# Four gate and value blocks of the first unit summed up before its scaling is known, and weight pieces 2 and 3 decoded earlier

## The chip, the cores and the metric

The kernel runs on one core of a Trainium2 chip. The metric is the device time of one execution in microseconds (us). TensorE (PE in the profile) multiplies matrices, VectorE (DVE), ScalarE (ACT) and GpSimd (POOL) do elementwise work, and SyncE (SP) issues the DMAs. Each engine works through its own list of instructions in order and waits on the others by semaphores.

## The reference

Windowed attention over 8 batches x 8 heads x 576 positions x 64, then an MLP with a gate over the 4608 rows of the attention's output:

```python
scores = where(mask, scale * q @ k.T, -1e9)      # 32 keys back, or 32 keys back in steps of 4
x      = softmax(scores) @ v                     # laid out as 4608 x 512
rms    = sqrt(mean(x * x, -1) + 1e-6)
xn     = x / rms * rms_g
g      = xn @ w_gate                             # 512 x 1536
out    = (g * sigmoid(g) * (xn @ w_val)) @ w_out # 1536 x 512
```

The weights arrive as 64-bit numbers, so the kernel has to make 32-bit ones of them.

## The kernel before

**Units and steps.** The 4608 rows are worked off in 16 units of 288 (`u`), with the features across the partitions. A unit's attention has 14 blocks of scores, `(u, c, i)`: c is a pair of heads (0 to 3), i a block of queries. The MLP has 12 blocks of 128 features (`j`), each with three steps: `gate` (tile g), `val` (tile v) and `proj` (tiles acc0 to acc3). The program is a list of steps. The opening has 25 of them, n = 0 to 24, with the attention of unit 0 and the first scores of unit 1. Then follows the main loop, in which t counts steps within all units: t = 3j + part, and unit 0 begins with t = 2.

**The order of work.** It is written out by hand. `later(dt, rank, fn)` puts a function into the step dt further on; at the head of each step `flush` calls what was put there, sorted by rank, and the matmuls of the step follow. The order of the calls is the order on each engine: nothing is rearranged later, and an instruction that waits holds up everything behind it on its engine.

**Weight pieces.** Gate, value and output weights come as 36 blocks of 128 x 512; two make one piece m: m = 0 is g0 and v0, m = 1 is g1 and v1, m = 2 is o0 and g2, m = 3 is v2 and o1, m = 4 is g3 and v3. A piece is loaded (L152), then `rebase` scales its high words into a new tile f (on POOL, L164, for m < 3, on ACT, L166, from then on), and then DVE makes the bits right. For m < SIGNS these are three operations, `shift` (L172), `low` (L175) and `sign` (L179). From SIGNS on there are two, `rest` (L184) and `whole` (L188), and for them POOL first clears the high words but for their sign, in place (L169), after `rebase` has read them. STEPS gives how many of these DVE operations each opening step has, and REBASES the opening steps with a rebase; in unit 0's part of the main loop every step has one operation, but for t = PAUSE.

**Unit 0's scaling.** Of each row the root of the mean square is needed. ACT copies the attention's output into xraw_c (L426; DVE does it for two blocks of c = 3), squares it (L445), POOL multiplies xraw_c by rms_g (L447), and POOL or DVE adds up the squares (L451). PE then sums over partitions (rps, L551), DVE adds 1e-6 (L558), POOL takes the power (L559), DVE spreads it over a diagonal (rd, L583), PE broadcasts it (bps, L593), and DVE multiplies xraw into xn (L604) and copies the factor to `root` (L598). One block, j = 0, doesn't wait for that: `start` (steps in FIRST) sums its g and v over the unscaled xraw, and DVE applies the root to g before the tanh (L683) and to the product (L704). L684 is the tanh, L689 finishes the gate, L702 multiplies with v.

**PSUM.** g and v of block j lie in two banks that alternate: g of block j + 1 takes the bank of v of block j, and v of block j + 1 that of g. So a `gate` may begin only when DVE has read the last v but one, by L702. `busy` are matmuls without use (L765), which keep PE occupied in the opening.

Of the kernel before, what the change touches and what calls it, by code (L numbers as in the profile page):

```python
# [9 lines left out]
F32 = mybir.dt.float32  # L10
# [4 lines left out]
ALU = mybir.AluOpType  # L15
# [5 lines left out]
P = 128  # L21
U = S // 2
# [3 lines left out]
QB = 96  # L26
# [8 lines left out]


LAG, OUT, LATER = 4, 2, 1
STEPS = (0,) * 6 + (1, 0) * 2 + (1,) * 4 + (0,) * 9 + (2, 1)
REBASES = 5, 9, 21, 23
BUSY = 5, 2  # L40
SIGNS = 4
SPLITS = 5, 31, 35

PAUSE = 31

ORDER = [(0, 0, "q"), (0, 1, "q"), (0, 0, "v"), (0, 2, "q"), (0, 0, "w"), (0, 1, "v"), (0, 3, "qv"), (0, 2, "v"),
         (0, 0, "g"), (0, 0, "w"), (0, 0, "w"), (1, 0, "qv")]
SECOND = 14, 18, 22
ZEROS = 19, 23, 26
FIRST = {19: (("g", 0), ("g", 1)), 20: (("g", 2),), 22: (("g", 3), ("v", 0), ("v", 1)),  # L50
         23: (("v", 2), ("v", 3))}


SCORES = {1: (-3, -2, 0, 1, 3, 4, 6, 7, 9, 10, 12, 13, 15, 16),
# [20 lines left out]
def attn_moe(ctx: ExitStack, tc: tile.TileContext, qk_in, v_in, w_gate, w_val, w_out, rms_g, outT):  # L75
# [560 lines left out]
    def weight(kind, u, j):  # L636
        return wts[kind, j] if u else single(kind, j)

    def three(out, wt, cc, x, start, stop, late_lo=False):
        if not isinstance(x, tuple):  # L640
            PE.matmul(out, wt[:, cc, :], x, start=start, stop=stop)  # L641
            return
        (wh, wl), (xh, xl) = wt, x
        PE.matmul(out, wh[:, cc, :], xh, start=start, stop=False)  # L644
        rest = [(wh, xl), (wl, xh)]
        for k, (w, v) in enumerate(rest[::-1] if late_lo else rest):
            PE.matmul(out, w[:, cc, :], v, start=False, stop=stop and k == 1)  # L647

    first = {}

    def start(kind, c):

        if kind not in first:
            first[kind] = ps.tile([P, 512], F32, tag={"g": "acc1", "v": "acc3"}[kind], name=f"{kind}_0_0")
        three(first[kind][:, :U], weight(kind, 0, 0), c, xraw[0, c], c == 0, c == NC - 1)

    def bank(kind, j):
        return "gv"[(j + (kind == "v")) % 2]

    def group(kind, u, j):  # L660

        if u + j == 0:
            return first.pop(kind)
        out = ps.tile([P, 512], F32, tag=bank(kind, j), name=f"{kind}_{u}_{j}")
        for c in range(NC):
            three(out[:, :U], weight(kind, u, j), c, xs[u][c], c == 0, c == NC - 1)
        return out

    def gate(u, j):
        g_ps = group("g", u, j)
        if u == 0:
            used.append(("g", j))
        g = g_ps[:, :U]

        def tanh():
            nonlocal g
            t = (sb.tile([P, U], F32, tag="hhi", name=f"h_{j}", bufs=2) if u == 0 else
                 sb.tile([P, U], F32, tag="th", name=f"th_{u}_{j}", bufs=1))  # L680
            if u + j == 0:
                g = sb.tile([P, U], F32, tag="hhi", name="g_first", bufs=2)
                V.tensor_tensor(out=g, in0=g_ps[:, :U], in1=root[0], op=ALU.mult)  # L683
            A.activation(out=t, in_=g, func=AF.Tanh, scale=0.5)  # L684
            gv[u, j] = t

        def silu():
            t = gv[u, j]
            V.scalar_tensor_tensor(out=t, in0=t, scalar=1.0, in1=g, op0=ALU.add, op1=ALU.mult)  # L689

        later(1, 0 if u + j else 0.65, tanh)
        later(1, 0.8, silu)
        return g_ps[:, U:U + 2 * QB]

    def val(u, j):
        v_ps = group("v", u, j)
        if u == 0:
            used.append(("v", j))

        def prod():  # L700
            t = gv[u, j]
            V.tensor_tensor(out=t, in0=t, in1=v_ps[:, :U], op=ALU.mult)  # L702
            if u + j == 0:
                V.tensor_tensor(out=t, in0=t, in1=root[0], op=ALU.mult)  # L704

        def parts():
            t = gv.pop((u, j))
            if u == 0:
                hs[u, j] = t
                return  # L710
            hi = sb.tile([P, U], F32R, tag="hhi", name=f"hhi_{u}_{j}", bufs=2)
            lo = late[0].tile([P, U], F32R, tag="hlo", name=f"hlo_{u}_{j}", bufs=2)
            A.copy(out=hi, in_=t)  # L713
            (V if (u, j) == (NU - 1, NJ - 1) else G).tensor_tensor(out=lo, in0=t, in1=hi, op=ALU.subtract)  # L714
            hs[u, j] = (hi, lo)

        later(1 if u + j else 2, 0, prod)
        later(1 if u + j else 2, 0.5, parts)
        return v_ps[:, U:U + 2 * QB]
# [42 lines left out]
    def busy(n):  # L762

        for _ in range(n):
            PE.matmul(busy_ps, ones, ones[:, None, :].to_broadcast([P, 4, P]), start=True, stop=True)  # L765
# [31 lines left out]
    for n in range(ends):  # L797
        decode(STEPS[n])
        if n in REBASES:
            later(0, 8, ahead)  # L800
        flush()
        t_ps = None
        if "t" in events.get(n, {}):
            t_ps = ps.tile([P, 512], F32, tag="gv"[n % 2] if n < nb + LAG else "acc0", name=f"t_first_{n}")[:, :2 * QB]
        s_tags = ("s", "acc0", "acc1") if n < nb else ("s", "acc0") if n < nb + LAG + OUT else ("s", "acc2")
        attend(t_ps, s_tag=s_tags[n % len(s_tags)], o_tag=("o", "acc2")[n % 2])
        if n < nb + LAG + OUT:
            busy(0 if n < 2 else BUSY[1] if n < nb + LAG - 1 else 1)
        for kind, c in FIRST.get(n, ()):
            start(kind, c)  # L810
        if n == ends - 1:
            gate(0, 0)
            val(0, 0)
        now[0] += 1

    prev = None
    for u in range(NU):
        for j in range(NJ):
            for part in range(0 if u + j else 2, 3):
                t = 3 * (u * NJ + j) + part  # L820
                if used and (t >= SPLITS[2] or part == 2 and SPLITS[0] <= t < SPLITS[1]):
                    later(0, 6, lambda: split_weight(*used.pop(0), V if t < SPLITS[1] or t % 2 else G, t >= SPLITS[2]))
                if u == 0:
                    decode(t != PAUSE)
                    if t == PAUSE:
                        later(0, 8.9, ahead)
                opening = len(ops) <= 2
                flush()
                if opening and not late:
                    early.close()  # L830
                    late.append(ctx.enter_context(tc.tile_pool(name="late", bufs=2)))
                if part == 0:
                    free = gate(u, j)
                elif part == 1:
                    free = val(u, j)
                else:
                    if prev is not None:
                        proj(*prev)
                    prev = (u, j)
                    free = None  # L840
                    if "t" in events.get(now[0], {}):
                        free = ps.tile([P, 512], F32, tag=bank("g", j), name=f"t_{u}_{j}")[:, :2 * QB]
                attend(free, s_tag="acc2" if t < 4 else "s")
                now[0] += 1
    flush()
# [69 lines left out]
```

## Time and profile before

| | us |
|---|---|
| median of 3 runs | 1125.83 |
| the three runs | 1125.37, 1125.83, 1130.24 |
| the profiled execution | 1130.38 |
| its span, first to last instruction | 1128.6 |
| PE busy in it | 1115.5 (99%) |
| DVE, ACT, POOL busy | 781.5, 700.9, 602.3 |

In the profile, a row of the timeline is start, duration, engine, line, operation, output and input tiles, and in brackets how long the engine was idle before and what it had waited for. A matmul in 32-bit precision is two records. L numbers are lines of the kernel before; in the changed one all lines behind the table of constants stand one further down (two from the loop over the opening steps on).

### The profile page before, as it was taken

How to read it: one execution, taken by the hardware profiler on the slowest of the kernel's cores; microseconds unless marked ns; L12 is line 12 of the kernel's file. 1: busy time of each engine (PE TensorE's matmuls, PEld its weight loads, DVE VectorE, ACT ScalarE, POOL GpSimd, SP SyncE). 2: the span in 40 equal slices, each digit the busy share in tenths (PEclk: the TensorE clock that was granted, in tenths of full speed). 3: DMA queues.
4: the chain of work that ended last, by engine and by line, in shares of the span. 5: the costliest groups of instructions: out<-in, count | busy, mean ns of one | idle time of the engine just before them, and what ended most of it. 6: DMA issues, size and time to landing. Idle time of an engine off the chain costs nothing.

```text
span 1128.6 us, 25810 instructions
## 1 busy us (share of the span) xinstructions
PE 1115.5 (99%) x8362; PEld 1086.6 (96%) x8362; DVE 781.5 (69%) x2838; ACT 700.9 (62%) x2579; POOL 602.3 (53%) x1050
## 2 busy tenths in 40 slices
PE   8999999999999999999999999999999999999998
PEld 6787999999999999999999999999999999999998
DVE  7789768758687675867758587685867767586412
ACT  6696576757567575766757666575766757576311
POOL 7423576646566554655646556564655646475211
PEclk9899999999999999999999999999999999999999
DMA  9666212303122121311313122121312212120000
GB/s 246 165 226 228 71 43 61 96 27 98 42 76 67 31 82 40 93 52 41 93 30 91 39 74 62 36 85 39 96 42 60 82 34 80 42 80 15 6 17 21
DMA packets 61544, 82.19 MB, mean 73 GB/s; under 512 B 7298, under 2 KB 41090, under 8 KB 61410
## 3 DMA queue, kind: packets, MB, share of 16 engines
q1 hardware_dynamic: 61410, 80.54, 24.2%
q8 instruction: 67, 1.10, 0.4%
q14 instruction: 67, 0.55, 0.2%
HBM read 71.08 MB, written 9.44 MB: 71 GB/s over the span
## 4 chain that ended last, share of the span: by engine, by line
PE 93%; DVE 3%; DMA 2%; ACT 1%; issue 1%; POOL 0%; SPq 0%; POOLq 0%; DVEq 0%; ACTq 0%
PE acc L647 16%; PE g L647 16%; PE v L647 16%; PE acc L644 9%; PE v L644 9%; PE g L644 9%; PE s L506 3%; PE o L494 3%; PE acc L641 2%; PE v L641 2%; PE g L641 2%; PE o L495 1%; PE t L481 1%; PE o L490 1%; PE v L481 1%; PE g L481 1%
## 5 line engine op out<-in xcount | busy, mean ns | idle before, releaser
L714 POOL TENSOR_TENSOR hlo<-th,hhi 128x288 fp32r<-128x288 f32 x179 | 145.3, 812 | 198.2 <-ACT hhi L713 148.4
L647 PE MATMUL acc<-hhi,lo 128*128 128x288 f32 x720 | 212.4, 295 | 0.0
L409 POOL TENSOR_SCALAR t<-t,sum 72x72 f32<-72x72 f32 (+3 forms) x414 | 153.4, 382 | 75.6 <-DVE sum L403 62.9
L647 PE MATMUL g<-xhi,lo 128*128 128x288 f32 x612 | 180.3, 295 | 0.0
L647 PE MATMUL v<-xhi,lo 128*128 128x288 f32 x612 | 180.2, 294 | 0.0
L713 ACT CAST hhi<-th 128x288 fp32r<-128x288 f32 x180 | 78.1, 434 | 153.4 <-DVE th L702 150.4
L393 ACT ACTIVATE t<-t,sum 96x128 f32<-96x128 f32 (+3 forms) x448 | 166.1, 375 | 10.3 <-DVE sum L382 9.8
L684 ACT ACTIVATE th<-g 128x288 f32<-128x288 f32 x180 | 73.8, 410 | 107.4 <-PE g L647 89.3
L321 POOL TENSOR_TENSOR vlo<-vt,vhi 128x128 fp32r<-128x128 f32 x182 | 86.1, 473 | 101.3 <-ACT vhi L317 87.4
L647 PEld LDWEIGHTS acc<-hhi,lo 128*128 128x128 f32 x720 | 135.4, 188 | 0.0
L439 DVE TENSOR_TENSOR xraw<-o,xraw 64x72 f32<-64x72 f32 (+1 forms) x364 | 99.2, 273 | 50.4 <-ACT xraw L429 44.4
L689 DVE SCALAR_TENSOR_TENSOR th<-th,g 128x288 f32<-128x288 f32 x180 | 80.5, 447 | 71.4 <-ACT th L684 67.5
L647 PEld LDWEIGHTS g<-xhi,lo 128*128 128x128 f32 x612 | 115.1, 188 | 0.0
L647 PEld LDWEIGHTS v<-xhi,lo 128*128 128x128 f32 x612 | 115.1, 188 | 0.0
L644 PE MATMUL g<-xhi,hi_g 128*128 128x288 f32 x357 | 111.4, 312 | 0.8 <-DVE th L702 0.8
L644 PE MATMUL acc<-hhi,hi_o 128*128 128x288 f32 x360 | 110.7, 307 | 0.0
L702 DVE TENSOR_TENSOR th<-th,v 128x288 f32<-128x288 f32 x180 | 81.5, 453 | 38.0 <-PE v L647 30.0
L647 PE MATMUL acc<-hlo,hi_o 128*128 128x288 f32 x360 | 106.5, 296 | 0.0
L429 ACT COPY xraw<-o 64x72 f32<-64x72 f32 (+1 forms) x364 | 94.1, 258 | 11.7 <-PE o L495 9.6
L377 DVE TENSOR_TENSOR t<-s,mask 96x256 f32<-96x256 f32 (+3 forms) x182 | 66.8, 367 | 47.7 <-PE s L506 42.3
L351 POOL TENSOR_TENSOR ks<-qk,ks 128x288 fp32r<-128x288 f32 (+2 forms) x104 | 99.6, 973 | 0.0
L647 PE MATMUL g<-xlo,hi_g 128*128 128x288 f32 x322 | 94.9, 295 | 0.0
(192 smaller groups left out, 3565.5 us busy)
## 6 DMA issues: line engine op xcount, KB each, us to landing
qk<-in_qk_dram SPq DMA_DIRECT2D x60, 288.0 KB, 2.8
vt<-in_v_dram SPq DMA_DIRECT2D x196, 64.0 KB, 1.8
qk<-in_qk_dram SPq DMA_DIRECT2D x30, 352.0 KB, 3.1
out_dram<-ot SPq DMA_DIRECT2D x64, 144.0 KB, 1.9
qk<-in_qk_dram SPq DMA_DIRECT2D x30, 304.0 KB, 2.8
raw<-in_w_gate_dram SPq DMA_DIRECT2D x12, 512.0 KB, 6.1
raw<-in_w_val_dram SPq DMA_DIRECT2D x12, 512.0 KB, 5.2
raw<-in_w_out_dram SPq DMA_DIRECT2D x12, 512.0 KB, 4.2
```

The lines of the kernel that those rows point to most:

```text
L321: G.tensor_tensor(out=vl, in0=vs.pop(b), in1=vh, op=ALU.subtract)
L351: ek.tensor_tensor(out=ks[:, 1, :nkt], in0=kr, in1=ks[:, 0, :nkt], op=ALU.subtract)
L393: A.activation(out=t[:nq, a, :n], in_=t[:nq, a, :n], func=AF.Exp, scale=-1.0, bias=sm[:nq, a, 0:1], accum_out=sm[:nq, a, 1:2] if u or i % ...
L409: (V if u == 0 and (c, i) > (NC - 1, 0) else G).tensor_scalar(out=t[:nq, a, :n], in0=t[:nq, a, :n], scalar1=sm[:nq, a, 3:4], scalar2=1.0, ...
L429: A.copy(out=to[a * D:(a + 1) * D], in_=o[a * D:(a + 1) * D, (2 + a) * nq:(3 + a) * nq])
L439: V.tensor_tensor(out=to[rows], in0=o[rows, a * nq:(a + 1) * nq], in1=to[rows], op=ALU.add)
L644: PE.matmul(out, wh[:, cc, :], xh, start=start, stop=False)
L647: PE.matmul(out, w[:, cc, :], v, start=False, stop=stop and k == 1)
L689: V.scalar_tensor_tensor(out=t, in0=t, scalar=1.0, in1=g, op0=ALU.add, op1=ALU.mult)
L702: V.tensor_tensor(out=t, in0=t, in1=v_ps[:, :U], op=ALU.mult)
L713: A.copy(out=hi, in_=t)
L714: (V if (u, j) == (NU - 1, NJ - 1) else G).tensor_tensor(out=lo, in0=t, in1=hi, op=ALU.subtract)
```

## The change

In the opening, `start` now also sums g and v of block j = 1 over the unscaled xraw, in PSUM banks v and g, which that block would have had anyway. FIRST spreads the sixteen matmuls over steps 14 to 24. The `busy` matmuls stop with step 13. In the main loop, `gate(0, 1)` and `val(0, 1)` issue no matmuls; DVE applies the root to g of block 1 (L684 there) and POOL to its product (L705 there). Pieces 2 and 3 are decoded in the short form (SIGNS = 2) and within the opening (STEPS, REBASES); the main loop resumes with piece 4 at t = 4. Transposes of the steps 14 to 17 and of t = 2 use other PSUM banks.

```diff
-STEPS = (0,) * 6 + (1, 0) * 2 + (1,) * 4 + (0,) * 9 + (2, 1)
-REBASES = 5, 9, 21, 23
-BUSY = 5, 2
-SIGNS = 4
+STEPS = (0,) * 6 + (1, 0) * 2 + (1,) * 4 + (0,) * 5 + (1, 1, 0, 0, 1, 1)
+REBASES = 5, 9, 18, 21
+BUSY = 5, 2, 14
+SIGNS = 2
...
-PAUSE = 31
+RESUME, PAUSE = 4, 30
...
-FIRST = {19: (("g", 0), ("g", 1)), 20: (("g", 2),), 22: (("g", 3), ("v", 0), ("v", 1)),
-         23: (("v", 2), ("v", 3))}
+FIRST = {14: ("g00",), 15: ("v00", "g10"), 16: ("v10", "g01"), 17: ("v01", "g11"), 18: ("v11", "g02"),
+         19: ("v02", "g12"), 20: ("v12",), 22: ("g03", "v03"), 23: ("g13",), 24: ("v13",)}
+AHEAD = {("g", 0): "acc1", ("v", 0): "acc3", ("g", 1): "v", ("v", 1): "g"}
...
-    def start(kind, c):
+    def start(kind, j, c):
...
-        three(first[kind][:, :U], weight(kind, 0, 0), c, xraw[0, c], c == 0, c == NC - 1)
+        three(first[kind, j][:, :U], weight(kind, 0, j), c, xraw[0, c], c == 0, c == NC - 1)
...
-        if u + j == 0:
-            return first.pop(kind)
+        if u == 0 and (kind, j) in AHEAD:
+            return first.pop((kind, j))
...
-            if u + j == 0:
-                g = sb.tile([P, U], F32, tag="hhi", name="g_first", bufs=2)
+            if u == 0 and j < 2:
+                g = sb.tile([P, U], F32, tag="th", name=f"g_first_{j}", bufs=1)
                 V.tensor_tensor(out=g, in0=g_ps[:, :U], in1=root[0], op=ALU.mult)
...
-            if u + j == 0:
-                V.tensor_tensor(out=t, in0=t, in1=root[0], op=ALU.mult)
+            if u == 0 and j < 2:
+                (G if j else V).tensor_tensor(out=t, in0=t, in1=root[0], op=ALU.mult)
...
-            t_ps = ps.tile([P, 512], F32, tag="gv"[n % 2] if n < nb + LAG else "acc0", name=f"t_first_{n}")[:, :2 * QB]
+            t_ps = ps.tile([P, 512], F32, tag="gv"[n % 2] if n < BUSY[2] else ("s", "acc0")[n % 2],
+                       name=f"t_first_{n}")[:, :2 * QB]
...
-        if n < nb + LAG + OUT:
-            busy(0 if n < 2 else BUSY[1] if n < nb + LAG - 1 else 1)
-        for kind, c in FIRST.get(n, ()):
-            start(kind, c)
+        if 1 < n < BUSY[2]:
+            busy(BUSY[1])
+        for kind, j, c in FIRST.get(n, ()):
+            start(kind, int(j), int(c))
...
-                    decode(t != PAUSE)
+                    decode(t >= RESUME and t != PAUSE)
...
-                        free = ps.tile([P, 512], F32, tag=bank("g", j), name=f"t_{u}_{j}")[:, :2 * QB]
+                        free = ps.tile([P, 512], F32, tag=bank("g", j) if t > 2 else "acc0", name=f"t_{u}_{j}")[:, :2 * QB]
```

The table of steps moves instructions on three engines. Three places follow, each before and then changed. The numbers at the end of a tile's name only keep tiles apart.

POOL from step 17 to the main loop's first steps, with the waits in brackets (`waits DVE` stands for a semaphore that DVE raises). sq_0 collects the squares; raw_140 and f_515 (f_539 before) are piece 2, raw_366 piece 3, raw_449 piece 4; rst is the root. Before:

```order
L447 TENSOR_SCALAR xraw_2_410<-xraw_2_410,gs 128x288 [waits Activation_49]
L451 TENSOR_TENSOR sq_0_335<-sq_0_335,sq_2_497 128x288 [waits Pool_49]
L260 MEMSET qk_1_118 64x608 [waits Pool_49]
L260 MEMSET qk_1_118 64x608
L447 TENSOR_SCALAR xraw_3_494<-xraw_3_494,gs 128x288 [waits Activation_49,Pool_49]
L164 TENSOR_SCALAR f_539<-raw_140 128x1024 [waits DMAHW6_49,DMAHW5_49]
L559 TENSOR_TENSOR rst_563<-rst_563,mhalf 96x3 [waits DVE_49]
```

POOL in the changed kernel:

```order
L448 TENSOR_SCALAR xraw_2_410<-xraw_2_410,gs 128x288 [waits Activation_49]
L452 TENSOR_TENSOR sq_0_335<-sq_0_335,sq_2_500 128x288 [waits Pool_49]
L165 TENSOR_SCALAR f_515<-raw_140 128x1024 [waits DMAHW6_49,DMAHW5_49]
L170 TENSOR_SCALAR raw_140<-raw_140 128x1024 [waits Pool_49]
L261 MEMSET qk_1_118 64x608 [waits Pool_49]
L261 MEMSET qk_1_118 64x608
L448 TENSOR_SCALAR xraw_3_497<-xraw_3_497,gs 128x288 [waits Activation_49,Pool_49]
L170 TENSOR_SCALAR raw_366<-raw_366 128x1024 [waits DMAHW2_49,DMAHW1_49,Activation_49]
L560 TENSOR_TENSOR rst_573<-rst_573,mhalf 96x3 [waits DVE_49]
```

The rebase of piece 2 has moved ahead of the last xraw, and two clearings (L170) are new ahead of the power.

DVE from step 18 to step 21: the last two copies out of the attention, the scores' maxima (ISA rows) and the last sum of squares. Before:

```order
L426 COPY xraw_3_494<-o_3_1_501 64x72 x2
L426 COPY xraw_3_494<-o_3_3_521 64x72 x2
L382 ISA t_0_0_533,sum_90<-s_0_0_529,mask 96x128
L382 ISA sum_90 96x1
L382 ISA t_0_0_533,sum_90<-s_0_0_529,mask 96x128
L382 ISA sum_90 96x1
L451 TENSOR_TENSOR sq_0_335<-sq_0_335,sq_3_536 128x288
```

DVE in the changed kernel:

```order
L427 COPY xraw_3_497<-o_3_1_504 64x72 x2
L185 SCALAR_TENSOR_TENSOR raw_140<-raw_140 128x1024
L427 COPY xraw_3_497<-o_3_3_530 64x72 x2
L189 SCALAR_TENSOR_TENSOR f_515<-f_515,raw_140 128x1024
L383 ISA t_0_0_541,sum_90<-s_0_0_537,mask 96x128
L383 ISA sum_90 96x1
L383 ISA t_0_0_541,sum_90<-s_0_0_537,mask 96x128
L383 ISA sum_90 96x1
L452 TENSOR_TENSOR sq_0_335<-sq_0_335,sq_3_544 128x288
```

Both operations on piece 2 now stand among these, the first (L185, which reads what POOL's L170 wrote) ahead of the last copy.

DVE around t = 4, where h_648 is the product of block 1 and g_1, v_1 its sums. Before:

```order
L402 TENSOR_REDUCE sum_88<-sum_88 96x2
L403 RECIPROCAL sum_88<-sum_88 96x2
L382 ISA t_1_1_652,sum_89<-s_1_1_639,mask 96x128
L382 ISA sum_89 96x1
L382 ISA t_1_1_652,sum_89<-s_1_1_639,mask 96x128
L382 ISA sum_89 96x1
L689 SCALAR_TENSOR_TENSOR h_648<-h_648,g_1_634 128x288
L179 SCALAR_TENSOR_TENSOR f_572<-raw_366,f_572 128x1024
L702 TENSOR_TENSOR h_648<-h_648,v_1_663 128x288
```

DVE in the changed kernel:

```order
L403 TENSOR_REDUCE sum_88<-sum_88 96x2
L404 RECIPROCAL sum_88<-sum_88 96x2
L684 TENSOR_TENSOR g_first_649<-g_1_477,root 128x288
L383 ISA t_1_1_654,sum_89<-s_1_1_639,mask 96x128
L383 ISA sum_89 96x1
L383 ISA t_1_1_654,sum_89<-s_1_1_639,mask 96x128
L383 ISA sum_89 96x1
L690 SCALAR_TENSOR_TENSOR h_648<-h_648,g_first_649 128x288
L185 SCALAR_TENSOR_TENSOR raw_449<-raw_449 128x1024
L703 TENSOR_TENSOR h_648<-h_648,v_1_492 128x288
```

Ahead of the product of block 1 the last operation on piece 3 has given place to the first on piece 4, which reads what POOL's L170 wrote into raw_449; and that one stands behind ACT's rebase of piece 4, which on ACT stands behind the tanh of block 1 in both kernels.

More of the change, by code (lines that the diff above doesn't have):

```diff
@@ L649, in attn_moe @@
     first = {}
-    def start(kind, c):
-        if kind not in first:
-            first[kind] = ps.tile([P, 512], F32, tag={"g": "acc1", "v": "acc3"}[kind], name=f"{kind}_0_0")
-        three(first[kind][:, :U], weight(kind, 0, 0), c, xraw[0, c], c == 0, c == NC - 1)
+    def start(kind, j, c):
+        if (kind, j) not in first:
+            first[kind, j] = ps.tile([P, 512], F32, tag=AHEAD[kind, j], name=f"{kind}_0_{j}")
+        three(first[kind, j][:, :U], weight(kind, 0, j), c, xraw[0, c], c == 0, c == NC - 1)
     def bank(kind, j):
```

## The prediction

> **What bounds the kernel now.** I read the page first (PE busy 99% of the span), then granted clock and busy times by windows, then the chain of waits through the opening, then the timelines of the engines there.
>
> ```profile
> 25.35:28.76 3.41, 2.54 (x13) 1.45 (x12) 3.24 (x14) 2.62 (x13) 2.01 (x4) 1.00 1.04 151
> 28.76:32.17 3.41, 3.25 (x14) 2.83 (x14) 1.36 (x8) 2.01 (x8) 0.89 (x2) 0.50 1.08 309
> 32.17:35.58 3.41, 3.41 (x11) 2.59 (x10) 0.62 (x3) 1.01 (x3) 2.34 (x5) 0.50 1.03 146
> 45.00:52.00 7.00, 5.29 (x27) 4.41 (x28) 6.64 (x25) 6.81 (x25) 2.27 (x1) 1.00 0.40 151
> 52.00:60.00 8.00, 8.00 (x43) 6.57 (x43) 7.76 (x22) 7.41 (x23) 1.75 (x3) 1.00 0.76 262
> ```
>
> A row is a stretch, its length, the busy time of PE, PEld, DVE, ACT and POOL, PE's granted clock, and DMA. From 52 us PE is never idle, so there a matmul less would count in full. Before that it is idle at times, and from 28.76 to 35.58 this execution ran PE at half clock.
>
> ```profile
> 28.93 0.43 PE t_first L481 x2
> ...
> 29.93 0.85 PE busy L765 x2
> ...
> 33.83 1.90 PE g L641 x4
> 35.73 0.45 PE s L503 x4
> ...
> 38.20 1.26 POOL rst L559
> ...
> 49.68 1.94 PE acc L641 x8
> 51.62 0.17 PE t L481 x2
> 51.79 0.35 PE o L490 x2
> 52.14 1.94 PE g L641 x8
> ```
>
> ```profile
> 46.71 2.21 PE L641 MATMUL v<-xn,f 128*128 128x288 f32 x8 [1.76 <-ACT pt L464]
> ...
> 51.98 1.38 PE L641 MATMUL g<-xn,f 128*128 128x288 f32 x5
> ```
>
> The first fence is the chain that ended last, the second PE's timeline. Up to 36 us the chain runs over PE at half clock (four records of L641 take 1.90, later eight take 1.94). Then comes the root: sum of squares, rps, power, and DVE's scaling, up to g_first. At 46.71 PE has been idle for 1.76 us, and from there on the chain is PE. **So the change is judged by when g of block 2 can start**, before at 51.98. All that follows is the same matmuls, back to back.
>
> **The change part by part.** It removes the eight matmuls of g_1 and v_1 from the main loop: 16 records, 2 x 1.94 = 3.9 us of PE. That is a gain only if PE is what g_2 waits for. In the opening it removes 9 busy matmuls (0.43 each at half clock, 0.26 at full, by 0.85 for two: 2.3 to 3.8 us) and adds those eight. Their cover is the path of POOL and DVE below; with that gone they cost 3.9 less 2.3, 1.6 us.
>
> First term: the two places where weight work now stands ahead of the root.
>
> ```profile
> 31.28 0.51 POOL L447 TENSOR_SCALAR xraw<-xraw,gs 128x288 f32<-128x288 f32 x1 [3.92 <-ACT sq L445]
> 31.75 0.79 POOL L451 TENSOR_TENSOR sq<-sq,sq 128x288 f32<-128x288 f32 x1
> 32.60 1.14 POOL L260 MEMSET qk<- 64x608 f32 x2
> 35.23 1.12 POOL L164 TENSOR_SCALAR f<-raw 128x1024 f32<-128x1024 f32 x1
> ```
>
> ```profile
> L166 ACT ACTIVATE f<-raw x15: 1132/1168/1225, 38.2 to 110.6; 128x1024 f32<-128x1024 f32 x15
> L169 POOL TENSOR_SCALAR raw<-raw x14: 1125/1402/2348, 49.7 to 111.9; 128x1024 f32<-128x1024 f32 x14
> L184 DVE SCALAR_TENSOR_TENSOR raw<-raw x14: 1211/1226/1805, 52.1 to 113.0; 128x1024 uint32<-128x1024 uint32 x14
> L188 DVE SCALAR_TENSOR_TENSOR f<-f,raw x14: 1201/1216/2130, 53.5 to 115.6; 128x1024 uint32<-128x1024 uint32 x14
> ```
>
> ```profile
> 33.44 0.58 DVE L426 COPY xraw<-o 64x72 f32<-64x72 f32 x2 [1.23 <-PE o L490]
> 36.32 0.29 DVE L382 CUSTOM_DVE_ANT_0 t<-s,mask 96x128 f32<-96x128 f32 x1 [2.29 <-PE s L503]
> ...
> 36.74 0.45 DVE L451 TENSOR_TENSOR sq<-sq,sq 128x288 f32<-128x288 f32 x1
> ...
> 37.95 0.16 DVE L558 TENSOR_SCALAR rst<-rps 96x3 f32<-96x3 f32 x1
> ```
>
> ```profile
> 34.14 0.44 ACT L445 ACTIVATE sq<-xraw 128x288 f32<-128x288 f32 x1 [1.03 <-DVE xraw L426]
> 36.65 0.40 ACT L393 ACTIVATE t<-t,sum 96x128 f32<-96x128 f32 x1 [2.06 <-DVE sum L382]
> ...
> 37.34 0.18 ACT L393 ACTIVATION_READ_ACCUMULATOR t<-t,sum 96x1 f32 x1
> ```
>
> DVE's idle 1.23 and 2.29 us look like room for two operations of 1.2 us. But `rest` of piece 2 has to wait for POOL's clearing, and POOL gets to it only after xraw_2, the sum of squares and the rebase. With POOL's start kept at 31.28: sum of squares done 32.55, rebase 1.12, done 33.7, clearing at its shortest (DVE is waiting, not working) 1.13, done 34.85. DVE: `rest` 1.23 to 36.1. Queued behind it is the last copy, 0.58, to 36.7 (before: from 33.44). ACT's square, 0.44 and a tenth for the handovers, to 37.2; DVE meanwhile `whole`, 1.22, to 37.9, and the maxima (0.42 from 36.32 to 36.74), to 38.35. There the sum of squares starts: 1.6 us later than 36.74. rps follows on PE; the add (L558), though, stands behind the first block's sums, which wait for ACT: rebase of piece 3 (1.14) from 37.2 to 38.35, the exponentials 0.9 (36.65 to 37.52 before), then two short sums, so the add falls at about 39.65 against 37.95, and the power at 39.9 against 38.20. POOL's clearing of piece 3 (38.4 to 39.8 at the median 1.40) just fits ahead of it. **Plus 1.7.** Upper end: PE's added matmuls at half clock (steps 15 and 16) push POOL's start by up to 0.9, and a clearing at the longest row, 2.35, delays the power by another 0.9: plus 3.5. Lower end 0: that would need the clearing of piece 2 to be done by 33.44 less 1.23, which POOL's own rows exclude unless xraw_2 comes 2.6 us earlier. Against an execution shaped like the profiled one I take the middle of the two clocks, plus 2.2.
>
> If PE's clock stays full, before and changed differ more. Before, PE's pieces from 28.93 to 36.18 (the end of s) would take half their time, 3.6 us less; about 0.6 of that would go to waiting for ACT's copies between them (an estimate: two handovers and a copy like the 0.30 of pt below). So the scores would be there 3.0 us earlier, and the whole root with them. The changed kernel would gain at most a tenth or two from it, POOL and DVE being its bound. So **plus 4.7** against such an execution.
>
> Second term: from g_first to g_2.
>
> ```profile
> 45.10 0.44 ACT L684 ACTIVATE h<-g_first 128x288 f32<-128x288 f32 x1 [2.98 <-DVE g_first L683]
> 48.21 0.30 ACT L464 COPY pt<-g 128x192 f32<-128x192 f32 x1
> 48.41 1.17 ACT L166 ACTIVATE f<-raw 128x1024 f32<-128x1024 f32 x1
> ```
>
> ```profile
> 44.62 0.45 DVE L683 TENSOR_TENSOR g_first<-g,root 128x288 f32<-128x288 f32 x1
> ...
> 45.95 0.69 DVE L172 TENSOR_SCALAR f<-f 128x1024 uint32<-128x1024 uint32 x1
> ...
> 47.28 0.46 DVE L704 TENSOR_TENSOR h<-h,root 128x288 f32<-128x288 f32 x1
> 47.66 1.22 DVE L175 SCALAR_TENSOR_TENSOR f<-raw,f 128x1024 uint32<-128x1024 uint32 x1
> ...
> 49.84 1.22 DVE L179 SCALAR_TENSOR_TENSOR f<-raw,f 128x1024 uint32<-128x1024 uint32 x1
> 50.97 0.44 DVE L702 TENSOR_TENSOR h<-h,v 128x288 f32<-128x288 f32 x1
> ```
>
> Before, g_2 starts 6.9 us after g_first's end (45.07 to 51.98). DVE now loses L172, L175 and L179 there (0.69 + 1.22 + 1.22 = 3.1), and gains 0.45 for the root on g_1: g_first_1 ends 3.35 us after g_first (the root on the product ended at 47.74, 2.67 after; less 0.15 of waiting, plus two short sums 0.4 and the 0.45). From there it is one thread without slack: tanh 0.4, the copy pt 0.3, ACT's rebase of piece 4 1.17, POOL's clearing 1.13, DVE's `rest` 1.23, and behind it in DVE's queue the product of block 1, 0.44. With 0.3 for handovers that is 5.0, so g_2, whose bank v_1 leaves only with that product, starts 3.35 + 5.05 = 8.4 us after g_first: **plus 1.5**. At the clearing's median and longest it is 1.8 and 2.7; if `rest` didn't have to wait, PE would set g_2: acc of block 0 after the root on its product, 2.67 + 0.1, then 1.94 + 0.17 + 0.35 and handovers make 5.4, minus 1.5. I take plus 1.5, since DVE stands still while POOL clears.
>
> No cost: the product's root on POOL (0.8 by the 0.79 row of L451; used first by proj of block 1, three steps later); SP waiting for piece 2 ahead of the fourth pair's scores (not needed for ten steps); the decoding afterwards, which is one step earlier and as long; the transposes' other banks (step 15 then waits for the last maxima before, an estimated 0.4 us, in POOL's shadow).
>
> Sum: 1130.38 + 2.2 + 1.5 = 1134.1 for an execution like the profiled one. That one is 4.55 above the median and close to the third timed run (1130.24); the two others are about the 3.0 us and some more below that the half clock costs. I take the median for executions without it: 1125.83 + 4.7 + 1.5 = **1132.0**.
>
> **The rivals.**
>
> One of the two waits only: the other is hidden by something I have put too early or too late. 1125.83 + 1.5 to 4.7, about 1129. For it: each needs only about 1.5 us of slack. Against: both threads run over single queues in order.
>
> Not slower: POOL reaches piece 2's clearing before DVE would have to wait, and piece 4's before block 1's product. This decides if xraw_2's square comes 2.6 us earlier than in the profile; then PE's work is the bound, and g_2 starts 1.5 us sooner: 1124.3. For it: DVE's idle 1.23 and 2.29 us are there. Against: the 3.92 us POOL was idle before 31.28 ended with ACT's square, which nothing here brings forward.
>
> Full gain: the 3.9 us of matmuls and 2.3 us of busy ones both come off: 1125.83 - 6.2 = 1119.6. Against: PE was not the chain where the busy ones stood.
>
> The clock: 2.54 us of busy PE out of 3.41 were followed by 0.50 for 6.82 us. In the changed kernel PE has nothing to do for some 4 us between the scores at about t = 3 and the transposed block that waits for ACT, and 3 us ahead of g_2. If half clock then reaches into the stretch from g_2 on, where PE is the bound, 3.4 to 6.8 us at half clock cost 1.7 to 3.4 us: about 1135. Against: the 1.76 us ahead of v in the chain (46.71) cost no clock. The Trainium skill ("TensorE: Matmul & The Clock Gate", Part 1: The HAM clock gate) says that PE's clock is halved after an idle window of about 3.4 us and released after a busy one, windows running freely of the kernel; the trace agrees in that its stretch is two times 3.41 us long. By that rule this rival is the likely course, 1135, and the runs should scatter by where a window falls.
>
> **How the numbers follow.** Forecast 0.40 (its own range 1130 to 1135), the clock 0.20, one wait only 0.12, not slower 0.20, full gain 0.08. A measurement of this kernel tells about 0.5%, 5.6 us, from no change: below 1120.2 is faster, above 1131.5 slower. Slower: 0.7 of the forecast and the clock, 0.48; the same: the rest of it, one wait and not slower, 0.44; faster 0.08. Range 1123 to 1138: from a little below the not-slower case to the upper ends of the first term and the clock.
>
> **What would show it.** In the changed profile: DVE's L185 on piece 2 idle ahead of it for POOL's L170, and the last copy after it (right: later than 35.5); POOL's power at 39.5 or later (wrong: before 38.5); L185 on piece 4 waiting about 2.4 us for L170; PE idle ahead of g_2 with DVE's L703 as releaser, and g_2 at 55 or later (wrong: before 53); the clock in the windows between 44 and 60 us. The forecast falls if PE is not idle there, or if a queue after 60 us gives the time back.

## The result and the profile after

| kernel | median, us | range, us | ratio to before (95% interval) |
|---|---|---|---|
| before, beside it | 1126.46 | 1125.37 to 1130.24 | |
| changed | 1131.47 | 1129.37 to 1132.34 | 1.0041 (1.0030 to 1.0052) |

The change costs 5.0 us, 0.41%. That is under the 0.5% (5.6 us) that the prediction took as the bound of no change, and 0.5 us from its forecast of 1132.0. The forecast stood 6.2 us above the kernel before; with nine runs instead of three that kernel's median rose from 1125.83 to 1126.46. The profiled execution took 1131.1 us, its span was 1129.0.

DVE's timeline in the changed kernel (start, duration, engine, line, operation, and in brackets the idle time and its releaser):

```profile
32.07 0.60 DVE L427 COPY xraw<-o 64x72 f32<-64x72 f32 x2 [1.71 <-PE o L491]
35.59 1.23 DVE L185 SCALAR_TENSOR_TENSOR raw<-raw 128x1024 uint32<-128x1024 uint32 x1 [2.92 <-POOL raw L170]
36.85 0.58 DVE L427 COPY xraw<-o 64x72 f32<-64x72 f32 x2
...
46.64 0.45 DVE L684 TENSOR_TENSOR g_first<-g,root 128x288 f32<-128x288 f32 x1
...
49.76 0.43 DVE L684 TENSOR_TENSOR g_first<-g,root 128x288 f32<-128x288 f32 x1
...
53.21 1.23 DVE L185 SCALAR_TENSOR_TENSOR raw<-raw 128x1024 uint32<-128x1024 uint32 x1 [2.06 <-POOL raw L170]
54.35 0.45 DVE L703 TENSOR_TENSOR h<-h,v 128x288 f32<-128x288 f32 x1
```

POOL's and PE's in the same execution:

```profile
40.60 0.87 POOL L560 TENSOR_TENSOR rst<-rst,mhalf 96x3 f32<-96x3 f32 x1
```

```profile
34.06 0.41 PE L491 MATMUL o<-pt,v 72*128 72x144 f32 x2
...
54.86 2.21 PE L642 MATMUL g<-xn,f 128*128 128x288 f32 x8 [1.02 <-DVE h L703]
```

Both waits are there: L185 stands still for POOL's clearing (L170), 2.92 us ahead of the last copy and 2.06 us ahead of the product of block 1 (L703), for which PE waits 1.02 us with block 2's gate. The power starts at 40.60 (38.20 before), the gate at 54.86 (51.98). But 2.9 us at that gate are not the whole story: the profiled execution before was itself 3.9 us over its median.

### The profile page after: what moved, and what is told of

It reads as the page before. It is cut to its first block, busy times and chain, and to the rows that moved or that the text cites. A ratio compares the mean times of both kernels' runs of the same rounds, so it can differ in the third digit from the quotient of the medians.

```text
span 1129.0 us, 25789 instructions
## 1 busy us (share of the span) xinstructions
PE 1110.5 (98%) x8353; PEld 1083.2 (96%) x8353; DVE 778.0 (69%) x2837; ACT 700.9 (62%) x2579; POOL 603.1 (53%) x1053
## 4 chain that ended last, share of the span: by engine, by line
PE 93%; DVE 3%; POOL 1%; ACT 1%; issue 1%; DMA 1%; SPq 0%; POOLq 0%; ACTq 0%; DVEq 0%
PE acc L648 17%; PE v L648 17%; PE g L648 17%; PE acc L645 9%; PE v L645 9%; PE g L645 9%; PE s L507 3%; PE o L495 3%; PE acc L642 2%; PE v L642 2%; PE g L642 2%; PE o L496 1%; PE t L482 1%; PE v L482 1%; PE g L482 1%
## 5 line engine op out<-in xcount | busy, mean ns | idle before, releaser
L410 POOL TENSOR_SCALAR t<-t,sum 72x72 f32<-72x72 f32 (+3 forms) x414 | 152.2, 380 | 75.1 <-DVE sum L404 64.7
L703 DVE TENSOR_TENSOR th<-th,v 128x288 f32<-128x288 f32 x180 | 81.4, 452 | 37.7 <-PE v L648 29.7
```

The source lines that it names most:

```text
L410: (V if u == 0 and (c, i) > (NC - 1, 0) else G).tensor_scalar(out=t[:nq, a, :n], in0=t[:nq, a, :n], scalar1=sm[:nq, a, 3:4], scalar2=1.0, ...
```

## The experiments

Each short diff below is against the kernel named. "Ratio" is that of the run to the kernel before on the same chip.

### The kernel before, profiled again (e0_before)

No edit.

> The kernel before, unchanged, for a second profile: the first profiled execution (1130.38 us, granted clock 0.50 for 6.8 us between 28.8 and 35.6) lay 3.9 us over the median. Theory (the half clock stood on the path, 3.0 us of it, as the prediction's estimate has it): with no such stretch the power of POOL L559 comes at 35 to 36 instead of 38.20, block 2's gate at 48.5 to 49.5 instead of 51.98, and the time is 1126 to 1127. Rival (the half clock was off the path and the profiled execution was long for another reason): block 2's gate at 51 or later even at full clock. Should the stretch of half clock be there again, the times come out as in the first profile, and only the timed executions tell.

It took 1126.1 us. POOL and PE in that execution, and the span with the mean clock:

```profile
34.50 0.87 POOL L559 TENSOR_TENSOR rst<-rst,mhalf 96x3 f32<-96x3 f32 x1
```

```profile
30.34 0.48 PE L490 MATMUL o<-pt,v 72*128 72x144 f32 x2
...
33.55 0.67 PE L551 MATMUL rps<-inv,sq 128*96 128x2 f32 x6 [0.15 <-DVE sq L451]
...
47.90 2.10 PE L641 MATMUL g<-xn,f 128*128 128x288 f32 x8
```

```profile
core 0: 1124.3 us, clock 1.000
```

The theory holds, and the clock cost more than expected: the power is 3.7 us earlier than in the first profile, block 2's gate 4.1 us, the time 4.3 us (1130.38 to 1126.10). This profile is the one to compare with. The changed kernel's gate is then 7.0 us late, its time only 5.0.

### The two waits taken away (e1_first, e2_second, e3_both, e6_spread)

```diff
 e1_first (from the changed kernel)
-REBASES = 5, 9, 18, 21
+REBASES = 5, 9, 15, 21
 e2_second
-REBASES = 5, 9, 18, 21
+REBASES = 5, 9, 18, 21, 24
-        if m < len(REBASES) - 1:
+        if m < 3:
 e3_both: REBASES = 5, 9, 15, 21, 24, and the second line of e2_second
 e6_spread: as e3_both, but
-STEPS = (0,) * 6 + (1, 0) * 2 + (1,) * 4 + (0,) * 5 + (1, 1, 0, 0, 1, 1)
+STEPS = (0,) * 6 + (1, 0) * 2 + (1,) * 4 + (0,) * 3 + (1, 1, 0, 1, 0, 0, 1, 0)
+REBASES = 5, 9, 15, 19, 24
```

> The changed kernel with one number of its table other: the rebasing and clearing of piece 2 go back in front of POOL's wait for the second block's squares (the idle 3.94 us ahead of POOL L448 at 32.00 us in the changed kernel's trace). Theory (the first wait sets when the first unit's statistics end): DVE L185 on piece 2 no longer waits 2.92 us for POOL L170, the last copy comes by 2 to 2.5 us earlier, the power of POOL L560 too (from 8.5 us after POOL's xraw_2 to about 6.3), and the time is the changed kernel's 1131.5 less 2 to 2.5, about 1129. Rival (the wait only takes the place of another, such as the tail of unit 0 or the signs in DVE's queue): the wait goes, but the power comes within 0.8 us of where it was, and the time stays at 1131 to 1132.

> The changed kernel with the rebasing and clearing of piece 4 as a step of the table, right behind piece 3's, instead of behind the second block's unpacked numbers (DVE L185 on piece 4 waits 2.06 us there, and PE 1.02 us ahead of block 2's gate with DVE L703 as releaser). Theory (the second wait sets block 2's gate): DVE's wait of 2.06 us goes, PE's wait ahead of that gate falls under 0.2 us, the stretch from block 0's gate to block 2's falls from 7.8 us by 1.0 to 2.0, and the time is 1129.5 to 1130.5. Rival (PE's own matmuls of blocks 0 and 1 fill that stretch anyway, one at 2.93 us under a lower clock): the stretch stays within 0.5 us and the time at 1131 to 1132. Second rival (piece 4's rebasing put sooner delays ACT's exponentials or POOL's power): the power of POOL L560 comes 0.5 to 1.2 us later and the time is 1131 to 1133.

> Both edits at once: piece 2's rebasing ahead of POOL's wait for the second block's squares, piece 4's as a step of the table. Theory (the two waits follow each other on the path to block 2's gate, so their prices add): the time is 1131.5 less 2 to 2.5 less 1 to 2, 1127 to 1128.5, about the 1126.5 of the kernel before. Rival (one path only, the second hidden behind the first): no better than the better of the two edits alone. A third reading (the matmul order itself loses time, the waits are little): 1130 or more.

> The changed kernel with another table for the decoding alone: pieces 2 and 3 decoded at later steps, one operation of DVE at a time, with every clearing of POOL ahead of the POOL work of the block whose squares it would hold up, and piece 4's rebasing as a step of its own. No arithmetic is changed. Theory (the change loses by waits of DVE for POOL's clearing, and its matmul order by itself is at least as good): no DVE L185 waits over 0.3 us for POOL L170 after the first piece, the last copy comes 1 to 3.5 us earlier than in the changed kernel, block 2's gate at least 3 us earlier by unit 1's start, and the time 1124 to 1127, at or under the 1126.5 of before. Rival (the matmul order itself costs, since PE does the gate and value of blocks 0 and 1 in full either way and the root stands behind them): 1128 to 1131 with the waits gone.

| run | median, us | ratio (95% interval) |
|---|---|---|
| e1_first | 1131.16 | 1.0036 (1.0024 to 1.0049) |
| e2_second | 1129.57 | 1.0026 (1.0017 to 1.0035) |
| e3_both | 1130.18 | 1.0035 (1.0022 to 1.0047) |
| e6_spread | 1130.23 | 1.0030 (1.0018 to 1.0041) |

Only e2_second came out as its theory said: DVE's wait for the clearing of piece 4 is gone, PE's wait ahead of block 2's gate fell from 1.02 to 0.23 us, and the time by 1.9 (1.7 by the ratios). DVE and PE in it:

```profile
25.71 1.64 DVE L410 TENSOR_SCALAR t<-t,sum 72x72 f32<-72x72 f32 x2
...
50.32 1.22 DVE L185 SCALAR_TENSOR_TENSOR raw<-raw 128x1024 uint32<-128x1024 uint32 x1
```

```profile
51.95 2.21 PE L642 MATMUL g<-xn,f 128*128 128x288 f32 x8 [0.23 <-DVE h L703]
```

e1_first took the first wait away and won nothing that can be told from no change. Why is seen in its timelines, DVE's, POOL's and PE's:

```profile
25.38 2.70 DVE L410 TENSOR_SCALAR t<-t,sum 72x72 f32<-72x72 f32 x2
...
34.18 1.46 DVE L185 SCALAR_TENSOR_TENSOR raw<-raw 128x1024 uint32<-128x1024 uint32 x1
```

```profile
26.77 1.09 POOL L165 TENSOR_SCALAR f<-raw 128x1024 f32<-128x1024 f32 x1
27.95 1.11 POOL L170 TENSOR_SCALAR raw<-raw 128x1024 f32<-128x1024 f32 x1
```

```profile
28.43 0.32 PE L482 MATMUL t_first<-ident,t 72*72 72x72 f32 x2 [1.75 <-DVE sum L383]
...
29.00 1.17 PE L642 MATMUL v<-xraw,f 128*128 128x288 f32 x2
...
35.53 0.41 PE L491 MATMUL o<-pt,v 72*128 72x144 f32 x2
```

L185 no longer waits. But the rebase, and at its very end the clearing, now meet a pair of DVE's scalings (L410): 2.70 us, against 1.64 for the same pair in e2_second, where POOL does not have them there. PE waits 1.75 us, then runs 3.4 us at half clock (1.17 for two records instead of 0.65), and the last output starts at 35.53, later than in the changed kernel (34.06). The Trainium skill ("SBUF — State Buffer", Who interferes with whom) has a rule for the first of these: a tensor_scalar of VectorE can take the port pair that it shares with GpSimd, and whichever engine comes second is blocked. The 2.70 and 1.64 agree with that in direction; no run here separates the port from anything else that the two engines share.

So the waits were real, but cover lay right behind them: with the first gone, the last output waits for PE, which has the added matmuls and runs part of them at half clock. The power comes at 39.74 in e1_first and at 39.66 in e2_second, which still has that first wait of 2.92 us. e3_both, at 35.53 for the last output, says the same; its 1130.18 is what its third reading allowed (1130 or more). e6_spread missed its theory's 1124 to 1127: the pair of scalings again took 2.70 us, PE ran 3.4 us at half clock from 29.3 us on, the last output came at 35.00, and of the waits for POOL one of 1.20 us was left. In these three the new collision and the half clock came together with the removed wait, so none of them prices the wait by itself.

### The change in two halves (e4_matmuls, e5_decode)

```diff
 e4_matmuls (from the changed kernel: decoding as before)
+STEPS = (0,) * 6 + (1, 0) * 2 + (1,) * 4 + (0,) * 9 + (2, 1)
+REBASES = 5, 9, 21, 23
+SIGNS = 4
+RESUME, PAUSE = 2, 31
 e5_decode (from the kernel before: decoding as changed)
+STEPS = (0,) * 6 + (1, 0) * 2 + (1,) * 4 + (0,) * 5 + (1, 1, 0, 0, 1, 1)
+REBASES = 5, 9, 18, 21
+SIGNS = 2
+RESUME, PAUSE = 4, 30
-                    decode(t != PAUSE)
+                    decode(t >= RESUME and t != PAUSE)
```

> The changed kernel with the decoding's table, its counts of signs and its pauses as they were before: the moved gate and value matmuls alone. The four runs so far took the waits of DVE for POOL away and won 0.3 to 1.9 us of the 5 lost, and their mean granted clock was 0.995 to 0.998 where the kernel before has 1.000 in most executions. Theory A (the lost time is in the decoding's waits and what they leave behind): 1126 to 1127.5. Theory B (the moved matmuls leave PE idle behind the root, so that the clock drops to half in every execution and the unpacking stands bare there): 1129 to 1131.5, mean clock 0.998 or less in all executions.

> The kernel before with the change's decoding table, counts of signs and pauses, and its own matmul order: pieces 2 and 3 decoded sooner, nothing else. Theory A (the decoding's waits for POOL's clearing lose the time): 1130 to 1132, DVE L184 waiting about 2.9 us for POOL L169 ahead of the last copies. Theory B (the moved matmuls lose it): 1126 to 1128, mean clock 1.000 in most executions, since PE keeps its gate and value matmuls behind the root.

e4_matmuls: 1127.9 us, ratio 1.0007 (0.9998 to 1.0016). e5_decode: 1134.12 us, ratio 1.0052 (1.0038 to 1.0066), beside a kernel before of 1127.05. The decoding is the dear half, as theory A had it, though both times lie above that theory's ranges (by 0.4 and 2.1 us). DVE and POOL in e5_decode:

```profile
34.25 1.23 DVE L184 SCALAR_TENSOR_TENSOR raw<-raw 128x1024 uint32<-128x1024 uint32 x1 [3.40 <-POOL raw L169]
35.51 0.58 DVE L426 COPY xraw<-o 64x72 f32<-64x72 f32 x2
```

```profile
39.70 0.87 POOL L559 TENSOR_TENSOR rst<-rst,mhalf 96x3 f32<-96x3 f32 x1 [0.49 <-DVE rst L558]
```

The last output is at 31.00, 0.7 us after that of e0_before, the power 5.2 us after it: here the wait for POOL's clearing stands on the path without the moved matmuls, and half clock (from 36.1 to 43.0) adds to it. The decoding alone is dearer than with the moved matmuls, but the halves differ in one thing more: e4_matmuls has the changed kernel's buffer for g_first, e5_decode the old one, and the runs on that buffer below price it at some 2 us. Theory B's sign of the clock was no sign: the mean clock was 0.996 to 0.998 in every execution of e4_matmuls and 0.995 to 0.997 in every one of e5_decode. PE in e4_matmuls:

```profile
32.57 0.41 PE L491 MATMUL o<-pt,v 72*128 72x144 f32 x2
...
36.28 0.67 PE L552 MATMUL rps<-inv,sq 128*96 128x2 f32 x6 [0.97 <-DVE sq L452]
...
51.69 2.10 PE L642 MATMUL g<-xn,f 128*128 128x288 f32 x8
```

Without any new decoding the last output is 2.2 us later than before (30.34), the sums over partitions 2.7 us (33.55): between the last two outputs stand two pieces of 0.49 us where one useless matmul of 0.24 stood, and the root waits for those outputs. And yet this execution (1126.38 us, span 1124.6), whose gate of block 2 is 3.8 us late, ends 0.3 us after that of e0_before. It is the fastest of its eleven, but the time is won back in the trace itself, about half of it by what the last two runs below show.

### The clock by itself (e8_fill)

```diff
 (from the changed kernel)
+FILL = {20: 2, 21: 2, 22: 2, 23: 2, 24: 3, 25: 3, 26: 5}
...
+    def fill(n):
+        if n in FILL:
+            into = ps.tile([P, 512], F32, tag="o", name=f"fill_{n}")
+            for _ in range(FILL[n]):
+                PE.matmul(into, ones, ones[:, None, :].to_broadcast([P, 4, P]), start=True, stop=True)
...
+        fill(n)
...
+                if u == 0:
+                    fill(ends - 2 + t)
```

> The changed kernel with 19 more matmuls without use (128x512 of ones into a free bank, some 0.24 us each at full clock) in the places where PE waits for the root: behind the scores of steps 20 and 21, in steps 22 to 24 and at t = 2 and 3. No arithmetic is changed. Theory (half clock in every execution of the changed kernel, two windows of 3.41 us in the profiled one, is part of the loss): mean clock rises towards 1.000 and the time falls to 1129 to 1130.3. Rival (the half clock stands where PE waits anyhow, or begins ahead of step 20): 1131 to 1132.5 at a clock of 0.997 or 0.998, or the same time at a higher clock.

1131.52 us, ratio 1.0040 (1.0028 to 1.0052): on the median no gain. But the six executions fall in two groups. Four had a mean clock of 0.998 and took 1131.24 to 1132.20; two had 1.000 and took 1129.46 and 1129.81. So a stretch of half clock is worth some 2.1 us here (2.5 between the two groups of e7_late below), and the changed kernel, at 0.996 to 0.998 in all nine executions, has at least one each time; the kernel before was at 0.999 or 1.000 in 43 of the 46 executions timed beside the last five runs. Its own profile at full clock is the cleanest look at the changed order, with 19 matmuls more:

```profile
39.40 0.87 POOL L561 TENSOR_TENSOR rst<-rst,mhalf 96x3 f32<-96x3 f32 x1
```

```profile
45.44 0.45 DVE L685 TENSOR_TENSOR g_first<-g,root 128x288 f32<-128x288 f32 x1
...
52.07 1.23 DVE L186 SCALAR_TENSOR_TENSOR raw<-raw 128x1024 uint32<-128x1024 uint32 x1 [2.10 <-POOL raw L171]
```

```profile
53.72 2.21 PE L643 MATMUL g<-xn,f 128*128 128x288 f32 x8 [0.98 <-DVE h L704]
```

The power is 4.9 us after that of e0_before (34.50), the gate of block 2 5.8 us (47.90). The time of that execution, 1129.46, is 3.4 us after 1126.10.

### The matmuls placed where they hold up nothing (e7_late, e9_third)

```diff
 e7_late (from e4_matmuls)
+FIRST = {14: ("g00",), 15: ("g10",), 16: ("v00",), 19: ("g01", "v01"), 20: ("g02",), 22: ("g03", "v02", "v03"),
+         23: ("g11", "g12")}
+THEN = {3: ("g13", "v10", "v11"), 4: ("v12", "v13")}
...
                 flush()
+                for kind, jj, c in THEN.get(t, ()) if u == 0 else ():
+                    start(kind, int(jj), int(c))
 e9_third (from e7_late)
+SIGNS = 3
+RESUME, PAUSE = 5, 31
+                    decode(2 if t == 21 else t == 2 or t >= RESUME and t != PAUSE)
+                    if t == 4:
+                        later(0, 8.9, ahead)
+                    if t == 5:
+                        later(0, 6, begun.clear)
```

> The moved matmuls alone, with the decoding as before (like the run of the matmuls alone, 1127.9 us against 1127.05), but placed otherwise: of the sixteen of blocks 0 and 1, three stand in the steps 14 to 16 in place of two busy matmuls each, none among the last outputs of the attention (steps 17 and 18), the others behind them as before; the last five of block 1 stand in the main loop's t = 3 and 4. Theory C (the extra matmuls between the last outputs push the last output and with it the root back: last output at 32.57 against 30.34, sums over partitions at 36.28 against 33.55): the sums over partitions start by 34.0 again, the mean clock is 1.000 in most executions, and the time is 1126 to 1127, that of before, since DVE's product of block 1 sets block 2's gate in both. Theory D (the place does not matter, the root on two more tiles costs): 1127.5 to 1128.5.

> The kernel of the run with the matmuls placed late, and piece 3 in two operations: the first at t = 2, with POOL's clearing of it right behind the power, the second behind block 1's product at t = 5, one operation later than before until t = 21. No arithmetic is changed. Theory C (DVE's product of block 1, behind 3.1 us of work on piece 3, is what block 2's gate waits for once PE is relieved): the stretch from block 0's gate (end of L685) to block 2's gate falls from 6.9 us to 5.4 to 6.0, and the time to 1124.5 to 1126, under the kernel before. Rival (PE idles more ahead of that gate, the clock drops, or the late pieces hold up block 2's value): 1126.5 to 1129.

e7_late: 1124.01 us, ratio 0.9983 (0.9975 to 0.9991), faster than both kernels and 2 us better than theory C allowed. Against the place among the outputs that is 2.7 us by the ratios (1127.9 and 1124.0, each beside its own kernel before), part of it by the clock: nine of the twelve executions were at 0.999 or 1.000, none of e4_matmuls was. But theory C had put the gain at nothing, and it gave 2.6. Its sign, sums over partitions by 34.0, is not met in this run's profile, which has a stretch of half clock in the opening (35.54), but in that of e11_tile_back, with the same order at full clock (33.66, below). e9_third: 1125.96 us, ratio 0.9997 (0.9988 to 1.0005), within theory C's 1124.5 to 1126, but no better than before and 1.9 worse than e7_late. The stretch from g_first's end to block 2's gate, which that theory had falling to 5.4 to 6.0 us, is 7.56 us, against 7.60 in e7_late. Freeing DVE around block 1 did not pay; what the later pieces cost instead stays open.

### One buffer (e10_tile, e11_tile_back)

The word that was left over: in the changed kernel g_first lies in the buffer `th`, before in one of the two buffers `hhi`.

```diff
 e10_tile (from the kernel before)
-                g = sb.tile([P, U], F32, tag="hhi", name="g_first", bufs=2)
+                g = sb.tile([P, U], F32, tag="th", name="g_first", bufs=1)
 e11_tile_back (from e7_late)
-                g = sb.tile([P, U], F32, tag="th", name=f"g_first_{j}", bufs=1)
+                g = sb.tile([P, U], F32, tag=("hhi", "th")[j], name=f"g_first_{j}", bufs=(2, 1)[j])
```

> The kernel before with one word of the change: the scaled gate g_first of block 0 lies in the buffer th instead of one of the two buffers hhi. All instructions and their order stay. From unit 2 on the seven profiled kernels with the moved matmuls win back 1.0 to 3.5 us against the kernel before, the two without them nothing, and the only difference left there in the program is which of the two buffers hhi each later tile gets (one tile less has been taken from them). Theory E (the buffers do it): 1123.8 to 1125, and the later sums over partitions come 2 us or more sooner than in the kernel before by unit 15. Rival (it is how the engines' work meets after the opening): 1126.2 to 1127, as before.

> The kernel with the matmuls placed late (1124.0 us, the fastest so far), with g_first of block 0 in hhi again, as in the kernel before, and that of block 1 in th. No other change. Theory E (the buffers win back some 2.5 us in the later units): 1126 to 1127, and the matmuls' place alone gives nothing. Rival (the place of the matmuls does it): 1123.8 to 1124.5.

e10_tile: 1124.71 us, ratio 0.9986 (0.9977 to 0.9994). e11_tile_back: 1126.95 us, ratio 1.0004 (0.9993 to 1.0014). Both times as theory E said: this word alone wins 2.0 us in the kernel before (1.6 by the ratio), and taking it back costs e7_late 2.9 (2.4 by the ratios). What e7_late won it owes to the buffer; the place of the matmuls alone wins nothing (1126.95 against 1126.71), though it keeps the sums where they were:

```profile
33.66 0.67 PE L553 MATMUL rps<-inv,sq 128*96 128x2 f32 x6 [0.28 <-DVE sq L453]
```

Where it is won: the start of the sums over partitions of the second unit (u = 1) and of the last (u = 15), first in e0_before, then in e10_tile:

```profile
98.75 0.59 PE L551 MATMUL rps<-inv,sq 128*96 128x2 f32 x6
...
1049.92 0.59 PE L551 MATMUL rps<-inv,sq 128*96 128x2 f32 x6
```

```profile
99.04 0.59 PE L551 MATMUL rps<-inv,sq 128*96 128x2 f32 x6
...
1048.89 0.59 PE L551 MATMUL rps<-inv,sq 128*96 128x2 f32 x6
```

951.2 us against 949.9. The changed kernel needs 948.8 (106.28 to 1055.12), e4_matmuls 948.2, e5_decode, which has the old buffer, 951.7. In e10_tile the instructions and their order are those of before on every engine, and both profiles are at full clock. Between these two sums the gain is 1.3 us, and by the last unit they come 1.0 us sooner, less than the 2 us expected there. The traces show more when all of PE's matmuls from block 2's gate to the last one are taken. They are 8130 records, the same and in the same order in every kernel here. The steps from the start of one to the start of the next within the gate, value and projection blocks sum to 869.8 to 870.0 us in the four kernels with the old buffer, and to 868.1 to 868.5 us in the ten with the new one (870.0 in e0_before, 868.2 in e10_tile). All other steps sum to 201.2 to 204.3 us and do not divide the kernels that way. So the buffer changes PE's pace inside the blocks, by some 1.7 us in all, and not a wait. What makes one of the two ways in which later tiles alternate between the buffers quicker is not shown and stays open.

## Why the prediction was right, and where not

**What the path is.** Right: the waits, their places, releasers and rough sizes (2.92 us; 2.06 against 2.4 predicted), the copy after 35.5, the power after 39.5 (40.60), PE idle ahead of block 2's gate. The gate came at 54.86, 0.14 us short of the "55 or later" named. That a wait was there did not yet say what it was worth: the second is priced by e2_second (1.7 to 1.9 us), the first by no run alone.

**Choosing the median.** Right: e0_before at full clock (1126.10) lies at the median. The half clock's 3.0 us was mis-sized; it was 3.7 at the power.

**First term, plus 4.7 against such an execution.** Measured 4.9 (39.40 against 34.50). It is two errors that cancel: the waits' own 1.7 was 1.2 (39.40 against 38.20), the half clock's 3.0 was 3.7.

**Cover of the matmuls.** The step "their cover is the path of POOL and DVE below; with that gone they cost 3.9 less 2.3, 1.6 us" held for the forecast, but the price behind it was mis-sized: 2.2 us at the last output and 2.7 at the sums (e4_matmuls). That fits e1_first, e3_both and e6_spread, which won so little by taking the waits away.

**Second term, plus 1.5.** From the end of g_first to block 2's gate it is 7.83 us in e8_fill and 7.77 in the changed kernel (46.64 + 0.45 to 54.86), against 6.91 in e0_before: plus 0.9. The thread behind g_first_1 took 4.7 instead of 5.05 us (49.00 to 53.72), and g_first_1 ended 3.1 instead of 3.35 after g_first.

**"All that follows is the same matmuls, back to back."** They are the same, and back to back, but this is the step that failed: PE's same matmuls in the same order took about 2.4 us less after the opening (5.8 us late at the gate, 3.4 at the end, in e8_fill), and the line of the diff that does most of it, the buffer of g_first (1.6 to 2.0 us by e10_tile), was not priced at all. The rest, about a us in the steps between blocks, has no cause shown. The prediction had named time given back after 60 us as something by which the forecast would fall.

**The clock.** Kept as a rival, 0.20, against the forecast; it belongs in the sum. All executions of the changed kernel have it, at 2.1 us by e8_fill. In the two profiles 1.2 us of it are there at the power (40.60 against 39.40), where the prediction gave the changed kernel "a tenth or two". The stretches in the profile of the changed kernel, each with the 3.4 us ahead of it (length, busy PE, PEld, DVE, ACT, POOL, then PE's clock and DMA):

```profile
17.90:21.30 3.40, 1.61 (x13) 1.02 (x10) 2.99 (x13) 2.37 (x10) 3.30 (x4) 1.00 1.05 234
21.30:24.70 3.40, 3.40 (x16) 2.98 (x17) 1.83 (x7) 1.35 (x6) 1.55 (x5) 0.50 1.03 311
45.20:48.60 3.40, 0.68 (x4) 0.46 (x4) 2.96 (x13) 1.45 (x7) 0.00 (x0) 1.00 0.33 94
48.70:52.10 3.40, 3.37 (x10) 2.90 (x11) 2.30 (x11) 3.21 (x11) 0.04 (x1) 0.51 0.58 228
```

The second begins where the rival said, where PE waits for the copy pt; it stands ahead of block 2's gate, not behind it, and from g_first's end to that gate it cost nothing (7.77 us, 7.83 without it in e8_fill). The Trainium skill ("TensorE: Matmul & The Clock Gate", Part 1: The HAM clock gate) has the clock fall after an idle window; in these rows PE was busy for 0.68 and 1.61 of 3.4 us, and 2.54 in the first profile before, so the measurement goes further than the page: a window need not be idle.

**The sum.** 1126.1 plus 4.9, 0.9 and 2.1, less 2.4 is 1131.6, against 1131.47. It closes because the 2.4 is what is left over in e8_fill; only the buffer's part of it was measured by itself. The forecast had 4.7 and 1.5 and lacked the last two, which cancel to 0.3 us. The total was right partly by luck. Of the rivals "one wait only", "not slower" and "full gain" fell: in the changed kernel neither wait was hidden.

## What to carry to other kernels

A wait that is taken away is worth what the next limit leaves: price the cover behind it, here PE's added matmuls, before moving anything, and look at what else the moved work will meet (POOL's clearing beside DVE's scalings). Fill a gap with work of the gap's own length: matmuls that replace useless ones between outputs cost their full surplus. In a diff, every word that changes which buffer later tiles get is a change of all that follows, and is best timed alone: here it was worth some 2 us of 1126 and carried the fastest kernel, at 1124.0.

## What was not expected of the hardware

One buffer's alternation is worth 2.0 and 2.9 us over sixteen units with no instruction changed (e10_tile, e11_tile_back), and in the traces it is PE's pace inside the blocks that differs (870.0 against 868.2 us). PE's clock drops in steps of 3.41 us in kernels that never leave it idle for a whole such stretch (its longest wait around the two steps of the changed kernel is 2.42 us), and two such steps cost the kernel before 4.3 us between two of its executions. A pair of 72x72 scalings on DVE took 0.42 us alone, 1.64 with two operations of POOL beside it, and 2.70 with three and the start of a fourth.
